# Pooling the keys on VectorE by a strided sum, and splitting and transposing x two blocks ahead in the expert loop

## The chip, the cores and the metric

The kernel runs on one core of one Trainium2 chip. Its engines have their own instruction streams: TensorE (PE, its weight loads are listed as PEld), VectorE (DVE), ScalarE (ACT), GpSimd (POOL) and SyncE (SP), which here only issues transfers. The metric is the device time of one execution in microseconds (us), the median of several runs. Lower is better.

## The reference

Four batches of 12288 queries of 128 channels attend to keys that are pooled from an image of 384 x 32 pixels: each key is the mean of a window of 4 x 4 pixels, so there are 768 keys a batch. The result passes through a mixture of experts: a token whose skip score is positive goes through the expert with the largest gate logit, and the others stay as they are.

```python
kv_pool = kv.reshape(B, H // r, r, W // r, r, C).mean(axis=(2, 4))     # r = 4
kv_flat = kv_pool.reshape(B, -1, C) @ w_sr                             # keys and values
a = softmax(q @ kv_flat.T / sqrt(C));   x = a @ kv_flat                # 49152 rows in all
out = x.copy();   xc = x[x @ w_skip > 0];   e_idx = argmax(xc @ w_gate, axis=1)
for e in range(E):                                                     # 8 experts, F = 1024
    y[e_idx == e] = gate_w * (relu(xc @ w1[e]) @ w2[e])
out[x @ w_skip > 0] = xc + y
```

## The kernel before, in words

**Attention.** 384 tiles of 128 queries, 96 a batch, in an order written out by hand. In each pass of the tile loop the kernel emits, for tile t: the scores of t (`scores`, six matmuls, L580 to L582, into `s_ps`, of which there are two buffers), the product with the values for tile t - 6 (`attend`, L643), the TensorE transposes for t - 1 (L618), the row maximum of t on VectorE (`row_max`, L588), then on ScalarE the high half of the probabilities of t - 1 (`p_hi`, L597) and exp of t (`row_exp`, L593), and on VectorE the low half (`p_lo`, L601), after which SP issues a transfer that transposes both halves. Each product is kept exact by splitting an operand in a high and a low part. After every 12 tiles a job `route` is queued: it works out gate, expert and destination row of 12 x 128 tokens on VectorE and GpSimd (L690 to L774), with two small TensorE matmuls for ranks (L750, L751), and then issues 12 scatters (`scatter_rows`, L184) on GpSimd, two a tile, which write the rows to expert-sorted lists in DRAM (`scr`). GpSimd also makes the low half of the queries once in four tiles (L569).

**Keys of the next batch.** During tiles 0 to about 78 of a batch, SP loads the next batch's image in six blocks of 128 keys (`load_kv`): a block is a tile `kvt` of 128 partitions (one for each key) by 2048 elements, 4 image rows of 4 pixels of 128 channels. Four tiles after a block's last load its pooling (`pool_kv`) joins a queue, `pools`. Blocks join at tiles 13, 26, 39, 52, 65 and 78 of the batch, and each pass of the tile loop takes one step from the queue (two from tile 74 on). A step of `pool_kv` is one GpSimd addition of 128x256, in place, the last one of 128x128: eight additions to a block (L439, L441). At tile 84 `prep_kv` turns the pooled keys into the operands of the next batch. The last batch has no pooling. Writes of padding rows lie in the tiles from 84 on of each batch and throughout the last batch. For the first batch the six blocks are pooled in the prologue: five on VectorE by `pool_kv_first` (a reduce over a strided view in which the 16 pixels of a window are the innermost axis, L426), and block 3 on GpSimd by `pool_kv`.

**The experts.** The first group of 2048 tokens is worked off by `peel`, code without a loop, of which a piece is emitted in each pass after the last attention tile. Then comes a hardware loop (L990) over the other groups. A group is one expert's weights and four blocks (stages) s = 0..3 of 512 tokens. Each block: `up` in eight chunks c (three matmuls each, L266 to L268, then relu in two halves, L269 on ScalarE and L270 on VectorE), `down` (L282), and, in the next block, `finish` (transposes back, L290, addition on VectorE, L293, and four scatters to the output). `x_transpose(s)` splits the rows `xin[s]` into `x16` (one buffer: L253 to L256 of ScalarE and VectorE) and has SP issue a transfer that transposes it into `xT[s]` (L259), from which `up(s)` reads. The loop is staggered: the engines pass from stage to stage at their own pace, and `previous_stage_wait(engine)` marks the place where an engine waits until the previous stage is done on all engines. `load_w` (weights, block 0), `w_scale` (blocks 1 and 2: the weights' scale, 2 reduces of L194 in front), `split_w1` and `split_w2` prepare the next group's weights.

Inside a block the order is: `up` chunk 0; GpSimd and SP wait for the previous stage; chunks 1 to 3; `split_w2` (block 0); `finish` of the previous block; `x_transpose` of the next block; `load_w` (block 0); `load_x` for the previous block's buffer; chunks 4 to 7; the weights' scale and `split_w1`; VectorE and ScalarE wait for the previous stage; `down`.

Of the kernel before, what the change touches and what calls it, by code (L numbers as in the profile page):

```python
# [15 lines left out]
ALU = mybir.AluOpType  # L16
AX = mybir.AxisListType
# [7 lines left out]
def kernel(  # L25
# [11 lines left out]
    nc = tc.nc  # L37
    NR, C, RT, P = q.shape
# [3 lines left out]
    R = 4  # L42
# [4 lines left out]
    FC = FF // P  # L47
# [2 lines left out]
    WEXP = 1  # L50
    W2EXP = 13
    XEXP = 2
    XC = 4
    DL = 1
    K1, K2 = 3, 2
    XP = 3
    XP2 = 4
# [19 lines left out]
    NST = G // ST  # L77
# [89 lines left out]
    op = ctx.enter_context(tc.tile_pool(name="op", bufs=2))  # L167
# [4 lines left out]
    writes, first_writes, finished, ready, loaded, moved = [], [], [], [], [], []  # L172
# [38 lines left out]
    def split_w1(pool=False):  # L211
        nc.scalar.activation(out=w1_hi, in_=w1_raw, func=AF.Copy, scale=w_sc[:, 0:1])
        if pool:
            nc.gpsimd.tensor_scalar(out=w1_raw, in0=w1_raw, scalar1=w_sc[:, 0:1], scalar2=None, op0=ALU.mult)
            nc.gpsimd.tensor_tensor(out=w1_lo, in0=w1_raw, in1=w1_hi, op=ALU.subtract)
            return
        nc.vector.scalar_tensor_tensor(out=w1_lo, in0=w1_raw, scalar=w_sc[:, 0:1], in1=w1_hi, op0=ALU.mult,
                                       op1=ALU.subtract)
# [21 lines left out]
    def split_w2():  # L240
        nc.scalar.activation(out=w2_hi, in_=w2_raw, func=AF.Copy, scale=w_sc[:, 1:2])
        nc.vector.scalar_tensor_tensor(out=w2_lo, in0=w2_raw, scalar=w_sc[:, 1:2], in1=w2_hi,
                                       op0=ALU.mult, op1=ALU.subtract)
        nc.vector.tensor_copy(y_sc[:, 0:1], y_sc[:, 1:2])

    def x_transpose(s, pool=False):
        for t in range(TT):
            nc.scalar.activation(out=x16[:, 0, t, :], in_=xin[s][:, t, 0:C], func=AF.Copy,
                                 scale=xin[s][:, t, C + 2:C + 3])
        if pool:  # L250
            x = op.tile([P, TT, C], F32, name="o")
            nc.gpsimd.tensor_tensor(out=x, in0=xin[s][:, :, 0:C], in1=xin[s][:, :, C + 2:C + 3].broadcast_to([P, TT, C]),
                                    op=ALU.mult)  # L253
            nc.gpsimd.tensor_tensor(out=x16[:, 1, :, :], in0=x, in1=x16[:, 0, :, :], op=ALU.subtract)
        for t in () if pool else range(TT):
            nc.vector.scalar_tensor_tensor(out=x16[:, 1, t, :], in0=xin[s][:, t, 0:C],  # L256
                                           scalar=xin[s][:, t, C + 2:C + 3], in1=x16[:, 0, t, :],
                                           op0=ALU.mult, op1=ALU.subtract)
        nc.sync.dma_start_transpose(xT[s], x16.rearrange("p a t c -> p (a t c)"))  # L259

    def up(s, cs):
        hi, lo = (xT[s][:, i * TT:(i + 1) * TT, :].rearrange("p t x -> p (t x)") for i in range(2))
        for c in cs:
            sl = slice(c * P, (c + 1) * P)
            ps = alloc["h"]()
            nc.tensor.matmul(ps, w1_hi[:, sl], hi, start=True, stop=False)  # L266
            nc.tensor.matmul(ps, w1_hi[:, sl], lo, start=False, stop=False)  # L267
            nc.tensor.matmul(ps, w1_lo[:, sl], hi, start=False, stop=True)  # L268
            nc.scalar.activation(out=h["hi"][:, c, :], in_=ps, func=AF.Relu)  # L269
            nc.vector.scalar_tensor_tensor(out=h["lo"][:, c, :], in0=ps, scalar=0.0, in1=h["hi"][:, c, :],  # L270
                                           op0=ALU.max, op1=ALU.subtract)
# [15 lines left out]
    def finish(s):  # L287
        ps = alloc["x"]()
        for t in range(TT):
            nc.tensor.transpose(ps[:, t * P:(t + 1) * P], yTs[s % 2][:, t * P:(t + 1) * P], ident)  # L290
        o = op.tile([P, TT, C], F32, name="o")
        for t in range(TT):
            nc.vector.scalar_tensor_tensor(out=o[:, t, :], in0=ps[:, t * P:(t + 1) * P],  # L293
                                           scalar=xin[s][:, t, C:C + 1], in1=xin[s][:, t, 0:C],
                                           op0=ALU.mult, op1=ALU.add)
        for t in range(TT):
            scatter_rows(out, xin[s].bitcast(I32)[:, t, C + 1:C + 2], o[:, t, :], NT - 1, "out")
# [41 lines left out]
    def peel():  # L339
        for s in range(NST):  # L340
            for c in range(FC):
                up(s, [c])
                if s == 0 and c == 3:
                    split_w2()
                if s > 0 and c == 3:
                    finish(s - 1)
                    finished.append(s - 1)
                if c == (XP if s < NST - 1 else XP2):
                    x_transpose((s + 1) % NST)
                    if s >= NST - 2:  # L350
                        moved.append(True)
                if s == NST - 1 and c in (1, 3):
                    scale = w_scale() if c == 1 else scale
                    next(scale, None)
                yield
            if s == NST - 1:
                split_w1()
            for i, _ in enumerate(down(s)):
                if s == NST - 1 and i + FC == XP2:
                    x_transpose(0)  # L360
                    moved.append(True)
                yield
            yield

# [2 lines left out]
    with ExitStack() as p1:  # L367
# [47 lines left out]
        def pooled_out(b, k):  # L415
            if k == 0:
                pooled[b] = kprep.tile([P, KC, C], F32, name="pooled")
            return KVT.pop((b, k)), pooled[b][:, k, :]
# [11 lines left out]

        def pool_kv(b, k):
            t, o = pooled_out(b, k)
            f = t.rearrange("p r x -> p (r x)")
            n = R * R * C
            m = 2 * C
            while n > 2 * C:
                n //= 2
                for c in range(0, n, m):
                    nc.gpsimd.tensor_tensor(out=f[:, c:c + m], in0=f[:, c:c + m], in1=f[:, n + c:n + c + m], op=ALU.add)  # L439
                    yield  # L440
            nc.gpsimd.tensor_tensor(out=o, in0=f[:, 0:C], in1=f[:, C:2 * C], op=ALU.add)  # L441

        HK = NK // 2
        HC = KC // 2
# [465 lines left out]
        t = -1  # L910
# [68 lines left out]
    with ExitStack() as p2:  # L979
        alloc_h(p2.enter_context(tc.tile_pool(name="hp", bufs=1)))  # L980
        ps_h = p2.enter_context(tc.tile_pool(name="ps_h", bufs=4, space=PSUM))
        ps_y = p2.enter_context(tc.tile_pool(name="ps_y", bufs=1, space=PSUM))
        ps_x = p2.enter_context(tc.tile_pool(name="ps_x", bufs=2, space=PSUM))

        alloc.update(h=lambda: ps_h.tile([P, ST], F32, name="h_ps"), x=lambda: ps_x.tile([P, ST], F32, name="x_ps"),
                     y=lambda: ps_y.tile([P, ST], F32, name="y_ps"))
        alloc["w"] = alloc["x"]
        tc.prologue_barrier()
        order.__exit__(None, None, None)
        with tc.For_i(0, n_it, 1, hint_engines=(mybir.EngineType.PE,), iteration_sync="staggered") as i:  # L990
            for s in range(NST):
                prv = (s - 1) % NST
                with tc.manual_schedule():
                    up(s, range(0, 1))
                    for eng in (nc.gpsimd, nc.sync):
                        tc.previous_stage_wait(eng.engine)
                    up(s, range(1, 4))
                    if s == 0:
                        split_w2()
                    finish(prv)  # L1000
                    up(s, range(4, XC))
                    x_transpose((s + 1) % NST)
                    if s == 0:
                        load_w(i + 1)
                    load_x(load_start(i if s == 0 else i + 1), prv)
                    up(s, range(XC, FC))
                    if s == 1:
                        scale = w_scale()
                    if s in (1, 2):
                        next(scale, None)  # L1010
                    if s == NST - 1:
                        split_w1()
                    for eng in (nc.vector, nc.scalar):
                        tc.previous_stage_wait(eng.engine)
                    for _ in down(s):
                        pass
                if s < NST - 1:
                    tc.stage_boundary()
        finish(NST - 1)
# [28 lines left out]
```

## Time and profile before

| | |
|---|---|
| median of 3 runs | 1989.95 us (1984.5 to 1991.75) |
| profiled execution | 1995.29 us, span 1992.7 us |
| mean granted TensorE clock | 0.965 |
| PE / DVE / ACT / POOL busy | 90% / 78% / 65% / 55% of the span |
| attention with its prologue, then the first expert group | 0 to about 1116 us, then to about 1209 us |
| expert loop | 1209.6 to about 1985 us |

The span runs from the first to the last instruction. The busy share is that of an engine over the whole span, and the stages differ: attention keeps four engines busy, the expert loop TensorE above all. In a row of a group of instructions stand line, engine, operation, tiles, the count, then the busy time and the mean of one in ns, and then the engine's idle time just before them with what ended most of it; "issue" means that the engine waited for nothing that the profile shows. A row of a table by stage has start and end, length, each engine's busy time with its count of instructions, the granted clock (1.00 is full speed), the share of DMA time and the GB/s moved.

### The profile page before, as it was taken

The numbers are of one execution on the slowest core, as the hardware profiler recorded it, in microseconds if no ns is written. First come the engines' busy times: TensorE is split into PE (matmuls) and PEld (weight loads), VectorE is DVE, ScalarE is ACT, GpSimd is POOL, SyncE is SP. The second block draws the span as 40 slices with busy tenths as digits, with TensorE's granted clock in tenths as the row PEclk, the third lists the DMA queues.
The fourth block names the chain that finished last, engine by engine and source line by source line (L and its number), as shares of the span: only waits on it lengthen the run. The fifth ranks groups of instructions, "written<-read, shape, count | busy, mean of one in ns | idle before, by whom it ended". The sixth has DMA issues, their size and how long they took to land. (4 is left out here: it accounts for less than half of the span.)

```text
span 1992.7 us, 42614 instructions
## 1 busy us (share of the span) xinstructions
PE 1802.1 (90%) x13955; PEld 1284.9 (64%) x13955; DVE 1560.5 (78%) x3222; ACT 1300.6 (65%) x2480; POOL 1095.2 (55%) x1372
## 2 busy tenths in 40 slices
PE   4999989999889998898988768999999999999997
PEld 3988878888878888787877523444444444444443
DVE  7889967999879888776778647777777777777776
ACT  3877867878768877676767534665656556565564
POOL 2378865888757878456556453333343333333334
PEclk9999989999999999888999879999999999999999
DMA  7999978999879999688988523333333333333333
GB/s 178 202 196 211 210 161 178 200 179 191 155 145 188 214 186 210 140 184 176 190 181 174 113 79 86 92 91 90 90 94 107 95 94 88 95 90 93 89 89 90
DMA packets 620915, 284.60 MB, mean 143 GB/s; under 512 B 502113, under 2 KB 570849, under 8 KB 620769
## 3 DMA queue, kind: packets, MB, share of 16 engines
q1 hardware_dynamic: 599264, 244.30, 59.6%
q0 software_dynamic: 21504, 38.43, 6.8%
q8 instruction: 82, 1.34, 0.3%
q14 instruction: 65, 0.52, 0.1%
HBM read 90.60 MB, written 78.64 MB: 85 GB/s over the span
## 5 line engine op out<-in xcount | busy, mean ns | idle before, releaser
L184 POOL DMA_INDIRECT out_dram<-o,xin x288 | 300.3, 1043 | 512.4 <-DVE o L293 435.5
L270 DVE SCALAR_TENSOR_TENSOR h_lo<-h_ps,h_hi 128x512 f16<-128x512 f32 x544 | 343.4, 685 | 174.9 <-ACT h_hi L269 174.9
L588 DVE TENSOR_REDUCE nm<-s_ps 128x1 f32<-128x768 f32 x384 | 363.7, 947 | 138.5 <-PE s_ps L582 73.9
L593 ACT ACTIVATE p_sb<-s_ps,nm 128x768 f32<-128x768 f32 x384 | 347.0, 904 | 187.1 <-DVE nm L588 152.3
L184 POOL DMA_INDIRECT scr<-rows,di x384 | 393.3, 1024 | 137.5 <-issue 108.1
L643 PE MATMUL acc_ps<-v_hi,pt 128*128 128x138 f16 x3072 | 331.5, 228 | 48.9 <-DVE rs L651 23.1
L643 PEld LDWEIGHTS <-pt 128*128 128x128 f16 x4608 | 286.3, 100 | 121.6 <-issue 120.3
L269 ACT ACTIVATE h_hi<-h_ps 128x512 f16<-128x512 f32 x544 | 299.3, 595 | 44.6 <-PE h_ps L268 21.1
L601 DVE SCALAR_TENSOR_TENSOR p<-p_sb,p 128x512 f16<-128x512 f32 x384 | 315.9, 823 | 1.8 <-ACT p L597 0.6
L643 PE MATMUL acc_ps<-v_lo,pt 128*128 128x138 f16 x1536 | 302.6, 227 | 1.0 <-issue 1.0
L580 PE MATMUL s_ps<-k_hi,q_hi 128*128 128x384 f32 x768 | 300.3, 391 | 2.3 <-issue 2.3
L581 PE MATMUL s_ps<-k_lo,q_hi 128*128 128x384 f32 x768 | 266.1, 347 | 4.3 <-issue 4.1
L582 PE MATMUL s_ps<-k_hi,q_lo 128*128 128x384 f32 x768 | 265.6, 346 | 2.6 <-issue 2.6
L597 ACT ACTIVATE p<-p_sb 128x512 f16<-128x512 f32 x384 | 242.4, 631 | 6.0 <-DMA pt<-p 3.0
L266 PE MATMUL h_ps<-xT,w_hi 128*128 128x512 f16 x544 | 206.6, 380 | 26.1 <-issue 26.1
L285 ACT ACTIVATE yT<-y_ps,y_sc 128x512 f32<-128x512 f32 x68 | 46.7, 687 | 276.6 <-PE y_ps L282 212.3
L268 PE MATMUL h_ps<-xT,w_lo 128*128 128x512 f16 x544 | 206.9, 380 | 0.0
L267 PE MATMUL h_ps<-xT,w_hi 128*128 128x512 f16 x544 | 206.8, 380 | 0.0
L282 PE MATMUL y_ps<-h_hi,w_hi 128*128 128x512 f16 x544 | 206.2, 379 | 0.0
L282 PE MATMUL y_ps<-h_hi,w_lo 128*128 128x512 f16 x544 | 206.2, 379 | 0.0
L282 PEld LDWEIGHTS <-w_hi 128*128 128x128 f16 x1152 | 113.3, 98 | 134.3 <-issue 3.7
L282 PE MATMUL y_ps<-h_lo,w_hi 128*128 128x512 f16 x544 | 195.1, 379 | 0.0
(215 smaller groups left out, 3215.0 us busy)
## 6 DMA issues: line engine op xcount, KB each, us to landing
kvt<-in_kv_dram SPq DMA_DIRECT2D x96, 256.0 KB
q_sb<-in_q_dram SPq DMA_DIRECT2D x96, 256.0 KB
out_dram<-rows SPq DMA_DIRECT2D x96, 256.0 KB
xin<-scr SPq DMA_DIRECT2D x75, 264.0 KB, 2.7
w_raw<-in_moe_w_dram SPq DMA_DIRECT2D x38, 512.0 KB, 3.8
scr<-pad SPq DMA_DIRECT2D x32, 264.0 KB
pt<-p SPq DMA_TRANSPOSE x384
scr<-rows,di POOLq DMA_INDIRECT x384
```

Of the source, the lines that this page charges most:

```text
L184: ins = nc.gpsimd.indirect_dma_start(out=dst, out_offset=bass.IndirectOffsetOnAxis(ap=ids, axis=0), in_=src, in_offset=None, bounds_check= ...
L269: nc.scalar.activation(out=h["hi"][:, c, :], in_=ps, func=AF.Relu)
L270: nc.vector.scalar_tensor_tensor(out=h["lo"][:, c, :], in0=ps, scalar=0.0, in1=h["hi"][:, c, :], op0=ALU.max, op1=ALU.subtract)
L282: nc.tensor.matmul(ps, w[:, c, :], h[x][:, c, :], start=(i == 0), stop=(i == len(terms) - 1))
L580: nc.tensor.matmul(s[:, h, :HK], q_hi, k_hi[:, sl], start=True, stop=False)
L581: nc.tensor.matmul(s[:, h, :HK], q_hi, k_lo[:, sl], start=False, stop=False)
L582: nc.tensor.matmul(s[:, h, :HK], q_lo, k_hi[:, sl], start=False, stop=True)
L588: nc.vector.tensor_reduce(out=NM[t], in_=S_PS[t][:, :, :HK], axis=AX.XY, op=ALU.max, negate=True)
L593: nc.scalar.activation(out=P_SB[t], in_=S_PS.pop(t)[:, :, :HK], func=AF.Exp, bias=NM.pop(t))
L597: nc.scalar.activation(out=P16[t][:, 0, :], in_=p_flat(t)[:, 0:KD * P], func=AF.Copy, scale=2.0 ** PEXP)
L601: nc.vector.scalar_tensor_tensor(out=p16[:, 1, :], in0=p_flat(t)[:, 0:KD * P], scalar=2.0 ** PEXP, in1=p16[:, 0, :], op0=ALU.mult, op1=ALU ...
L643: nc.tensor.matmul(ps[:, j % 2, :], w, v[a][:, k, :], start=(i == 0), stop=(i == len(AVL) - 1))
```

## The change

There are three parts. `pool_kv` becomes two VectorE reduces over the strided view, one for each half of the channels, in place of eight GpSimd additions; a block now takes two steps of the queue. In the loop, `x_transpose` is for the block after the next, and is emitted behind chunk 7, after the loads; VectorE's and ScalarE's wait for the previous stage moves up to before chunk 3, and TensorE gets the same wait there. In the peeled group, the x of the loop's second block is split and transposed too, inside the last block's `down`; the test that stood in that place was never true (i + 8 is never 4), and the transpose of the loop's first block stays at chunk 4.

```diff
-    XC = 4
...
             for i, _ in enumerate(down(s)):
-                if s == NST - 1 and i + FC == XP2:
-                    x_transpose(0)
-                    moved.append(True)
+                if s == NST - 1 and i == 1:
+                    x_transpose(1)
                 yield
...
         def pool_kv(b, k):
             t, o = pooled_out(b, k)
-            f = t.rearrange("p r x -> p (r x)")
-            n = R * R * C
-            m = 2 * C
-            while n > 2 * C:
-                n //= 2
-                for c in range(0, n, m):
-                    nc.gpsimd.tensor_tensor(out=f[:, c:c + m], in0=f[:, c:c + m], in1=f[:, n + c:n + c + m], op=ALU.add)
-                    yield
-            nc.gpsimd.tensor_tensor(out=o, in0=f[:, 0:C], in1=f[:, C:2 * C], op=ALU.add)
+            v = t.rearrange("p r (w c) -> p c (r w)", c=C)
+            m = C // 2
+            for c in range(0, C, m):
+                nc.vector.tensor_reduce(out=o[:, c:c + m], in_=v[:, c:c + m, :], axis=AX.X, op=ALU.add)
+                yield
...
                     up(s, range(0, 1))
                     for eng in (nc.gpsimd, nc.sync):
                         tc.previous_stage_wait(eng.engine)
-                    up(s, range(1, 4))
+                    up(s, range(1, 3))
+                    for eng in (nc.vector, nc.scalar, nc.tensor):
+                        tc.previous_stage_wait(eng.engine)
+                    up(s, range(3, 4))
                     if s == 0:
                         split_w2()
                     finish(prv)
-                    up(s, range(4, XC))
-                    x_transpose((s + 1) % NST)
                     if s == 0:
                         load_w(i + 1)
                     load_x(load_start(i if s == 0 else i + 1), prv)
-                    up(s, range(XC, FC))
+                    up(s, range(4, FC))
+                    x_transpose((s + 2) % NST)
                     if s == 1:
                         scale = w_scale()
                     if s in (1, 2):
                         next(scale, None)
                     if s == NST - 1:
                         split_w1()
-                    for eng in (nc.vector, nc.scalar):
-                        tc.previous_stage_wait(eng.engine)
                     for _ in down(s):
                         pass
```

## The prediction

> **What bounds the kernel now.** I read the page's busy times first, then tables of busy time by stage (start and end in us, length, then busy time of PE, PEld, DVE, ACT, POOL, the granted clock, DMA share and GB/s), then groups of instructions, waits and timelines inside the stages that the change touches.
>
> ```profile
> PE 1802.1 (90%) x13955; PEld 1284.9 (64%) x13955; DVE 1560.5 (78%) x3222; ACT 1300.6 (65%) x2480; POOL 1095.2 (55%) x1372
> ```
> ```profile
> 63.30:91.70 28.40, 28.40 (x316) 26.48 (x313) 25.78 (x47) 25.00 (x47) 12.28 (x17) 1.00 0.99 214
> 361.90:514.60 152.70, 143.96 (x1553) 131.91 (x1553) 144.31 (x260) 124.70 (x228) 130.83 (x174) 1.00 0.99 186
> 595.50:783.10 187.60, 175.75 (x1875) 160.72 (x1875) 170.25 (x312) 149.99 (x274) 151.10 (x204) 0.99 1.01 198
> 869.50:1009.50 140.00, 123.55 (x1241) 112.52 (x1240) 104.89 (x208) 100.20 (x182) 79.54 (x109) 0.93 0.91 187
> 291.50:331.40 39.90, 35.05 (x331) 32.19 (x332) 28.82 (x61) 26.37 (x48) 21.18 (x29) 0.88 0.86 168
> 557.00:595.50 38.50, 33.15 (x329) 29.85 (x330) 28.22 (x63) 26.21 (x48) 21.51 (x30) 0.96 0.82 159
> 253.40:265.60 12.20, 8.16 (x61) 7.19 (x59) 4.91 (x11) 4.75 (x10) 9.32 (x15) 0.72 0.84 162
> 521.40:533.30 11.90, 7.28 (x61) 6.42 (x61) 5.17 (x10) 4.78 (x10) 9.42 (x15) 0.86 0.63 122
> ```
>
> PE is the first limit: 90% busy, and the first row is twelve attention tiles at 28.40 us with PE busy all the time, 2.37 us a tile. I call twelve tiles (one routing job, twelve scatters) a row. The second and third lines are five and six rows in which GpSimd also pools the next batch's keys: 340.30/11 = 30.94 us a row, POOL and DVE nearly full. The fourth is four rows of the last batch, with no pooling: 35.00 us a row although POOL is busy only 57%, and the clock falls to 0.93. The next two are the first rows of batches 1 and 2, before pooling starts: 39.2 us on average. So in this kernel the rows *without* pooling are the slow ones, and the first question is why.
>
> Two stretches of GpSimd's timeline (start, us, then the instruction), and the waits of TensorE that fall behind the first:
>
> ```profile
> 891.69 1.08 POOL L184 DMA_INDIRECT scr<-rows,di  x1 [0.52 <-issue]
> 893.07 0.97 POOL L184 DMA_INDIRECT scr<-rows,di  x1 [0.30 <-issue]
> 894.35 0.97 POOL L184 DMA_INDIRECT scr<-rows,di  x1 [0.31 <-issue]
> 895.62 0.97 POOL L184 DMA_INDIRECT scr<-rows,di  x1 [0.30 <-issue]
> 896.89 0.98 POOL L184 DMA_INDIRECT scr<-rows,di  x1 [0.30 <-issue]
> 898.18 0.97 POOL L184 DMA_INDIRECT scr<-rows,di  x1 [0.30 <-issue]
> ```
> ```profile
> 386.82 0.97 POOL L184 DMA_INDIRECT scr<-rows,di  x1 [0.30 <-issue]
> 387.80 0.76 POOL L439 TENSOR_TENSOR kvt<-kvt 128x256 f32<-128x256 f32 x1
> 388.72 0.99 POOL L184 DMA_INDIRECT scr<-rows,di  x1 [0.17 <-issue]
> 390.02 0.97 POOL L184 DMA_INDIRECT scr<-rows,di  x1 [0.30 <-issue]
> 391.01 1.22 POOL L439 TENSOR_TENSOR kvt<-kvt 128x256 f32<-128x256 f32 x1
> ```
> ```profile
> 897.55 0.33 PE L580 MATMUL s_ps<-k_hi,q_hi 128*128 128x384 f32 x1 [1.03 <-issue]
> 899.25 0.67 PE L581 MATMUL s_ps<-k_lo,q_hi 128*128 128x384 f32 x1 [0.84 <-issue]
> ```
>
> Without pooling, six scatters follow one another every 1.28 us, and some 5 us after the run began TensorE stands still by pieces, put down to nothing that the profile shows. With pooling, each pair of scatters has an addition (L439) behind it, and no such stop follows. The profile does not say what the scatters hold up; that runs of six and stops go together is what I build on.
>
> The expert loop, from its first matmul to the end of its last block (17 groups of four blocks):
>
> ```profile
> 1209.61:1978.80 769.19, 746.62 (x3561) 354.80 (x3562) 589.46 (x1326) 452.96 (x917) 282.74 (x271) 1.00 0.36 93
> ```
> ```profile
> PE h_ps L266 <- issue: 26.1, 35, 3.5
> ```
> ```profile
> 1490.87 1.25 SPq L259 DMA_TRANSPOSE xT<-x  x1
> 1505.80 0.29 DVE L195 TENSOR_SCALAR w_dg<-ident,w_max 128x128 f32<-128x128 f32 x1
> ```
> ```profile
> 1494.45 0.38 PE L266 MATMUL h_ps<-xT,w_hi 128*128 128x512 f16 x1 [0.58 <-issue]
> 1506.13 0.38 PE L266 MATMUL h_ps<-xT,w_hi 128*128 128x512 f16 x1 [0.72 <-issue]
> ```
>
> TensorE is the bound here: 22.6 us idle of 769. The idle time sits at the first up matmul of a block (35 waits, 26.1 us, the 3.5 us of loop entry included): twice a group, once because the transpose of the next block's x was issued only 3.58 us before the block starts (1490.87 to 1494.45), once right after DVE's weight-scale work (1505.80), behind which stands DVE's wait for the previous stage.
>
> **The change, part by part.** My sum is made against the profiled run, 1995.29 us for a span of 1992.7; the median of the runs is 1989.95, so I subtract 5.3 at the end.
>
> *The additions that GpSimd loses.* The groups of the pooling stage 361.9 to 514.6, GpSimd first, then VectorE's there and (last) in the stage without pooling:
>
> ```profile
> L184 POOL DMA_INDIRECT scr<-rows,di x58 | 60.7, 1047 | 16.8 <-issue 12.1 <-POOL rows L774 4.4 <-PE acc_ps L643 0.2
> L439 POOL TENSOR_TENSOR kvt<-kvt 128x256 f32<-128x256 f32 x32 | 27.3, 860 | 0.2
> ```
> ```profile
> L601 DVE SCALAR_TENSOR_TENSOR p<-p_sb,p 128x512 f16<-128x512 f32 x60 | 54.8, 914 | 0.0
> ```
> ```profile
> L601 DVE SCALAR_TENSOR_TENSOR p<-p_sb,p 128x512 f16<-128x512 f32 x48 | 35.5, 740 | 0.0
> ```
>
> Each of the 18 blocks pooled inside the tile loop gives up seven additions of 0.86 us and one smaller, some 6.5 us of GpSimd. They all leave the path if GpSimd is not the bound, and they take two things with them. First, the gaps between the pairs of scatters. Pooling stood in 18 rows; the first (63.30 to 91.70, 17 POOL instructions) has hardly a scatter yet, so 17 rows lose their gaps. If these become like the rows without pooling, each costs 35.00 - 30.94 = 4.06 us more by the last batch's rows, or 39.2 - 30.94 = 8.3 by the first rows of batches 1 and 2. The latter carry the same key loads as the rows in question, but also the start of a batch; I take 4.06, since I can't take the start out of the others, and keep 8.3 for the range: 17 x 4.06 = **+69** (0 if GpSimd's run does no harm there; to +140). Second, VectorE's p_lo is 914 ns beside the additions and 740 without: 12 x 0.174 = 2.1 us of VectorE a row. That gain is already inside the 35.00.
>
> The Trainium skill ("SBUF — State Buffer", section "Who interferes with whom") says that a VectorE instruction with two SBUF inputs contends with a GpSimd instruction that reads SBUF, while a reduce never does. The 914 against 740 ns agree; taken alone, the rule would make the change a gain, which is rival B.
>
> *The reductions that VectorE gains.* The nearest rows are the reduces over the same strided view in the prologue:
>
> ```profile
> L426 DVE TENSOR_REDUCE pooled<-kvt 128x128 f32<-128x2048 f32 x3 | 10.8, 3596 | 8.3 <-DMA kvt<-in_kv_dram 8.3
> L426 DVE TENSOR_REDUCE part<-kvt 128x128 f32<-128x1024 f32 x2 | 3.8, 1898 | 0.4 <-DMA kvt<-in_kv_dram 0.4
> ```
>
> The new ones read 1024 elements a partition each, so 1.90 us, two to a block, in consecutive tiles. VectorE has 104.89/48 = 2.19 us of work per tile without pooling, TensorE needs 2.37: 0.18 to spare. Two reduces put VectorE 3.80 - 0.36 = 3.4 us behind. Behind them wait the row maximum (L588), then ScalarE's exp, then the free score buffer that TensorE needs. There are two such buffers, so TensorE can run about one tile's work ahead; with 2.1 us of lead, 1.3 us of the 3.4 shows: 17 x 1.3 = **+22** (0 to 3.4 x 17 = 58).
>
> By the Trainium skill ("VectorE: DVE Perf Modes", "The perf-mode tier table") a 1x pass over 2048 fp32 elements takes 2293 ns, so half of it about 1.15 us, an estimate; the row says 1.90 for this strided view, and by the page this term would be near nothing.
>
> *GpSimd no longer late at the end of a batch.*
>
> ```profile
> PE misc L750 <- POOL oh_all L723: 4.0, 1, 4.0
> ```
>
> In 253.40 to 265.60, two tiles took 12.20 us instead of 4.74 (11.90 in 521.40 to 533.30): TensorE's rank matmul waits 4.0 us for GpSimd, which is late from pooling, and the pipeline behind it empties. The same stop stands once in each of three batches. With pooling gone GpSimd is in time: 3 x 7 = **-21** (-22 to 0, if the routing is late for another reason).
>
> *The prologue's block.*
>
> ```profile
> 18.02 4.95 POOL L439 TENSOR_TENSOR kvt<-kvt 128x256 f32<-128x256 f32 x7 [13.14 <-DMA kvt<-in_kv_dram]
> ```
>
> This work ran beside VectorE's own reduces, which follow each other there with waits of 0.4 us; on VectorE it is two reduces of 1.90 in the chain to the first scores: **+3.5** (0 to 3.8).
>
> *The loop.* Issued a block earlier, the transposes are off the path, and the previous-stage wait no longer stands behind the weight scale. At stake is all idle time at L266 but the entry: 26.1 - 3.5 = 22.6, with a little at the weight loads, so **-22** (0 to -28). Against it: SP now issues the transpose behind the x load, and the single x16 buffer is held by the transpose of the block before, so ScalarE and VectorE can wait for it; SP's queue also carries the weight loads. *The entry:* a second transpose in the last peeled block needs rows that are loaded late:
>
> ```profile
> 1205.09 1.65 SPq L190 DMA_DIRECT2D xin<-scr  x2
> 1209.61 0.38 PE L266 MATMUL h_ps<-xT,w_hi 128*128 128x512 f16 x1 [3.49 <-issue]
> ```
>
> ```profile
> xin<-scr SPq DMA_DIRECT2D x75, 264.0 KB, 2.7
> ```
>
> The load (2.7 us from issue to landing, after 1205.09), the split and the transpose (3.58) end near 1212, so +3 once (0 to 5).
>
> Sum: 69 + 22 - 21 + 3.5 - 22 + 3 = +54.5; 1995.3 + 54.5 - 5.3 = **2044**.
>
> **The rivals.** **B, relief wins** (the other side): the scatters' run does no harm in these rows, because it hurts only where something else of the slow rows is there too (padding writes or a batch start). Then 69 is 0, and half of the 2.1 us of VectorE a row reaches TensorE: 22 - 17 x 1.05 = +4, with -21, -22 and +6.5: -32.5, **1957**. Its floor is VectorE full: 12 x 2.19 + 3.8 = 30.1 a row against 30.94, so -14 in place of +4: 1939. For it: POOL is 86% busy and p_lo slow in pooling rows. Against: of the two kinds of row without pooling one has key loads and the other has padding, and both stop. It decides from a run price under 1.9 us a row (32.5/17). **C, VectorE becomes the bound:** no harm from the runs, but the two reduces cost their full 3.4: 17 x (3.4 - 1.05) = +40 for +4, so +3.5: **1993**. The Trainium skill ("VectorE: DVE Perf Modes", "Rules for kernel authors") speaks for it: it calls the reduce the slowest VectorE operation on a hot path and advises restructuring. **D, the loop does not do what it says:** the forecast with its 22 us lost to the x16 buffer or SP's order: 2044 + 22 = **2066**.
>
> **Chances.** Forecast 0.49, D 0.10, B 0.28, C 0.13. Within 0.5% (10 us, about what a measurement of this kernel can tell from no change) lie 0.08 of C; the rest of C is split evenly. Faster 0.28 + 0.025 = 0.305, same 0.08, slower 0.49 + 0.10 + 0.025 = 0.615. The forecast's own range is 2008 (half the run's price) to 2085 (40 more, a run price of 6.4); B must be held down to 1950, and I leave out its lower third (0.09) and the dearest end of the run's price with D (0.1): 1950 to 2085.
>
> **What would show it.** Right: GpSimd's timeline shows runs of six scatters in 361 to 515, the same five rows take 175 or more instead of 152.7 with POOL less busy, and the granted clock dips there. B: those rows at 30 to 31 us each, no stop behind six scatters. C: ScalarE's exp waiting long for L588 beside the new reduces with no run near. The new reduces should read about 1.9 us; PE's wait for L723 should be gone; idle time at L266 should drop to the entry's. Wrong at the root I would be if the pieces of idle TensorE time in the last batch stem from something that the scatters only accompany.

## The result

The changed kernel takes 2064.15 us (median of 4 runs, 2063.22 to 2078.57), the kernel before 1990.85 (1984.5 to 1998.91): 3.85% slower, a ratio of 1.0385 with a 95% interval of [1.0335, 1.0436]. The forecast was 2044, between 1950 and 2085, slower. The profiled execution took 2078.57 us for a span of 2076.7, against 1995.29 and 1992.7.

One thing is needed to read the numbers behind this. The four later comparisons each set their kernels against the kernel before on one chip, and each met another chip. On two of these the kernel before took 1893 to 1895 us, on the other two 1992 and 2002, as in the first pair. What differs between them is the main finding of the experiments: in the second kind TensorE stops behind runs of scatters. I call them chips without and chips with stops. The names are for the condition alone: chip and time changed together from one comparison to the next, so the runs do not tell whether the condition belongs to the chip.

The busy times of the page after, and the table by stage of the changed kernel (columns as in the prediction: start and end, length, then PE, PEld, DVE, ACT, POOL, clock, DMA share, GB/s):

```profile
PE 1836.3 (88%) x13955; PEld 1315.3 (63%) x13955; DVE 1597.7 (77%) x3264; ACT 1328.5 (64%) x2484; POOL 966.0 (47%) x1220
```
```profile
365.30:595.40 230.10, 193.51 (x1903) 176.11 (x1901) 181.76 (x324) 151.34 (x277) 126.19 (x173) 0.92 0.78 152
670.70:897.90 227.20, 193.27 (x1886) 174.56 (x1885) 179.97 (x325) 150.69 (x275) 125.76 (x170) 0.92 0.82 166
973.50:1116.50 143.00, 127.79 (x1273) 116.74 (x1271) 105.14 (x210) 101.82 (x187) 83.62 (x116) 0.92 0.90 185
```

The first two rows are six rows of twelve tiles each with pooling, in batches 1 and 2: 38.35 and 37.87 us a row, where before it was 30.54 and 31.27. They now look like the third, the four rows of the last batch without pooling (35.75, before 35.00). The granted clock is 0.92 in all three. Every engine has a smaller share of the span than before. GpSimd's timeline in one run of scatters, then TensorE's instructions behind it that had to wait:

```profile
1033.53 1.07 POOL L183 DMA_INDIRECT scr<-rows,di  x1 [0.52 <-issue]
1034.91 0.97 POOL L183 DMA_INDIRECT scr<-rows,di  x1 [0.31 <-issue]
1036.18 0.97 POOL L183 DMA_INDIRECT scr<-rows,di  x1 [0.30 <-issue]
1037.45 0.97 POOL L183 DMA_INDIRECT scr<-rows,di  x1 [0.30 <-issue]
1038.73 0.97 POOL L183 DMA_INDIRECT scr<-rows,di  x1 [0.30 <-issue]
1040.00 0.97 POOL L183 DMA_INDIRECT scr<-rows,di  x1 [0.30 <-issue]
```
```profile
1039.31 0.27 PE L612 MATMUL acc_ps<-ident,p_sb 128*128 128x128 f32 x1 [1.02 <-issue]
1040.74 0.43 PE L576 MATMUL s_ps<-k_hi,q_lo 128*128 128x384 f32 x1 [0.80 <-issue]
1043.94 0.39 PE L637 MATMUL acc_ps<-v_hi,pt 128*128 128x138 f16 x2 [2.25 <-DVE rs L645]
```

These are the stops of the forecast. From the fourth scatter of the run on, TensorE halts twice between two matmuls of the same tile, for no reason that the profile shows; its third wait, of 2.25 us, is put down to VectorE's `rs`. TensorE is not the only engine that stands still:

```profile
1042.24 0.96 DVE L582 TENSOR_REDUCE nm<-s_ps 128x1 f32<-128x768 f32 x1 [5.49 <-PE s_ps L576]
```

By the order of the instructions this row maximum is that of the scores whose last matmul began at 1036.71 and took 0.34 us. VectorE starts it 5.2 us after that, and `rs` stands behind it. ScalarE has waited 3.97 us when it goes on at 1040.78. Behind the stop TensorE is slow as well: the granted clock is 1.00 from 1036.00 to 1038.00 and 0.52 from 1044.00 to 1047.00, and the pairs of L637 take 0.44 us there in place of 0.28.

The rest of the change as it came out is in the following lines. VectorE's pooling group and its low halves of the probabilities in 365 to 595; then the first scores' row maximum, before and after; then the loop's first and last block (the last of the kernel before, then both of the changed one, and its entry wait):

```profile
L434 DVE TENSOR_REDUCE pooled<-kvt 128x64 f32<-128x1024 f32 x12 | 23.4, 1953 | 0.0
...
L595 DVE SCALAR_TENSOR_TENSOR p<-p_sb,p 128x512 f16<-128x512 f32 x72 | 55.5, 771 | 0.0
```
```profile
34.28 0.96 DVE L588 TENSOR_REDUCE nm<-s_ps 128x1 f32<-128x768 f32 x1
```
```profile
37.80 0.96 DVE L582 TENSOR_REDUCE nm<-s_ps 128x1 f32<-128x768 f32 x1
```
```profile
1970.02 0.38 PE L266 MATMUL h_ps<-xT,w_hi 128*128 128x512 f16 x1
```
```profile
1319.64 0.58 PE L265 MATMUL h_ps<-xT,w_hi 128*128 128x512 f16 x1 [7.42 <-issue]
...
2052.18 0.38 PE L265 MATMUL h_ps<-xT,w_hi 128*128 128x512 f16 x1
```
```profile
PE h_ps L265 <- issue: 7.4, 1, 7.4
```

The reduce reads 1.95 us, p_lo 771 ns in place of 914, the prologue is 3.52 us longer, and the loop from its first to its last block takes 2052.18 - 1319.64 = 732.54 us instead of 1970.02 - 1209.61 = 760.41: 27.87 less. The only wait left at the first up matmul in the loop is its entry's. The loop starts 1319.64 - 1209.61 = 110.03 us later than before: 3.52 of it from the prologue and 7.42 - 3.49 = 3.93 from the entry, so 102.6 from the attention's tiles and the first expert group. That is where the time went. The profiled execution is the longest of the changed kernel's, 14 us above the median, so its stages are somewhat dearer than those of a usual one.

### The profile page after: what moved, and what is told of

It reads as the page before. It is cut to its first block, busy times and chain, and to the rows that moved or that the text cites. A ratio compares the mean times of both kernels' runs of the same rounds, so it can differ in the third digit from the quotient of the medians.

```text
span 2076.7 us, 42615 instructions
## 1 busy us (share of the span) xinstructions
PE 1836.3 (88%) x13955; PEld 1315.3 (63%) x13955; DVE 1597.7 (77%) x3264; ACT 1328.5 (64%) x2484; POOL 966.0 (47%) x1220
## 5 line engine op out<-in xcount | busy, mean ns | idle before, releaser
L183 POOL DMA_INDIRECT out_dram<-o,xin x288 | 295.7, 1027 | 494.6 <-DVE o L292 428.4
L637 PE MATMUL acc_ps<-v_hi,pt 128*128 128x138 f16 x3072 | 343.0, 233 | 108.9 <-DVE rs L645 67.0
L637 PEld LDWEIGHTS <-pt 128*128 128x128 f16 x4608 | 297.2, 102 | 189.9 <-issue 189.1
L268 ACT ACTIVATE h_hi<-h_ps 128x512 f16<-128x512 f32 x544 | 318.3, 597 | 51.1 <-PE h_ps L267 31.9
L637 PE MATMUL acc_ps<-v_lo,pt 128*128 128x138 f16 x1536 | 311.7, 232 | 4.7 <-issue 4.6
L574 PE MATMUL s_ps<-k_hi,q_hi 128*128 128x384 f32 x768 | 306.2, 399 | 4.5 <-issue 4.3
L595 DVE SCALAR_TENSOR_TENSOR p<-p_sb,p 128x512 f16<-128x512 f32 x384 | 289.9, 755 | 1.6 <-ACT p L591 1.0
L576 PE MATMUL s_ps<-k_hi,q_lo 128*128 128x384 f32 x768 | 270.0, 352 | 6.2 <-issue 6.2
L563 POOL TENSOR_TENSOR q_lo<-q_sb,q_hi 128x512 fp32r<-128x512 f32 x96 | 123.8, 1290 | 236.5 <-ACT q_hi L562 236.2
L637 PE MATMUL acc_ps<-v_hi,ptq 128*128 128x138 f16 x1536 | 189.6, 230 | 7.8 <-issue 7.5
```

What stands on the lines that cost most here:

```text
L183: ins = nc.gpsimd.indirect_dma_start(out=dst, out_offset=bass.IndirectOffsetOnAxis(ap=ids, axis=0), in_=src, in_offset=None, bounds_check= ...
L574: nc.tensor.matmul(s[:, h, :HK], q_hi, k_hi[:, sl], start=True, stop=False)
L576: nc.tensor.matmul(s[:, h, :HK], q_lo, k_hi[:, sl], start=False, stop=True)
L595: nc.vector.scalar_tensor_tensor(out=p16[:, 1, :], in0=p_flat(t)[:, 0:KD * P], scalar=2.0 ** PEXP, in1=p16[:, 0, :], op0=ALU.mult, op1=ALU ...
L637: nc.tensor.matmul(ps[:, j % 2, :], w, v[a][:, k, :], start=(i == 0), stop=(i == len(AVL) - 1))
```

## The experiments

My theory, R, was that runs of scatters stop TensorE and that GpSimd's additions had kept them apart. Its rival, V, was that the two reduces on VectorE cost the time and the scatters only accompany the stops.

**The parts alone.** The first kernel is the one before with the loop's part of the change, the second with the pooling's part.

```diff
 e1: before + x_transpose((s + 2) % NST) behind chunk 7, the moved waits, x_transpose(1) in the peeled group
 e2: before + pool_kv as two nc.vector.tensor_reduce a block
```

> The kernel before with the loop's part of the change alone (x two blocks ahead, the waits moved, the second transpose in the peeled group); keys still pooled on GpSimd. In the trace of the changed kernel the 67 block starts of the loop span 732.5 us instead of 760.4, and the loop's entry waits 7.4 us instead of 3.5. If the two parts add, this kernel is 28 - 4 = 24 us faster than before: about 1967. If the loop only runs faster because VectorE or the queues are left in another state by the attention, it is within 10 us of 1991.

> The kernel before with the pooling's part alone, prologue included. If the two parts add, 2064 + 24 = 2088. Below 2075 the parts would not be independent.

This was a chip without stops: the kernel before took 1893.54. The loop's part took 1869.31, ratio 0.9871 [0.9854, 0.9887], 24.2 us faster; the pooling's part 1922.52, ratio 1.015 [1.0133, 1.0167], 29.0 us slower. The loop's part is worth the 24 that were expected. The pooling's part costs 29 us instead of the nearly 100 expected from the first pair, and its rows without pooling, like those of the first kernel, don't stop. The two kernels by stage, six rows with pooling (the first kernel's second row: four rows without):

```profile
313.60:498.10 184.50, 174.80 (x1895) 160.79 (x1893) 176.48 (x313) 149.36 (x277) 160.24 (x211) 1.00 1.00 194
822.90:940.90 118.00, 115.93 (x1262) 107.06 (x1260) 108.43 (x210) 100.07 (x186) 84.36 (x113) 1.00 1.09 222
```
```profile
326.90:526.50 199.60, 179.50 (x1899) 165.28 (x1897) 185.18 (x325) 150.67 (x278) 132.09 (x174) 0.97 0.91 181
```

Here a row costs 30.75 us with GpSimd's pooling, 33.27 with VectorE's and 29.50 with none. The exchange of poolings costs 33.27 - 30.75 = 2.5 us a row, by the same rows of two kernels. Against the rows without pooling VectorE's two reduces cost 33.27 - 29.50 = 3.8 us a row, nearly all of their 3.9 us, so no sign is left that the two score buffers hide any of it; GpSimd's additions cost 1.25. These two figures are less sure, since the rows without pooling also lack the key loads and have writes of padding rows.

**One scatter a tile, and filler additions.** Both change the spacing of the scatters in the changed kernel and leave its reduces as they are.

```diff
 e3: after, with 4 buffers for rowp in place of 3 (SNAPR is 27)
-                if j % 2 == 0 and j > 0 and r < LASTR - 1:
+                if (j > 0 if r < SNAPR else j % 2 == 0 and j > 0) and r < LASTR - 1:
                     yield
 e4: after, with two scratch tiles junk
...
                 if j % 2 == 0 and j > 0 and r < LASTR - 1:
+                    nc.gpsimd.tensor_tensor(out=junk[0], in0=junk[0], in1=junk[1], op=ALU.add)   # 128x256
                     yield
```

> The changed kernel with one scatter a tile in place of two (a step of the routing job behind each scatter, in the first 27 rows; one more buffer for rows, since a row is held longer). Theory R (runs of scatters stop TensorE): the runs of six are gone, and with them a stop of about 5.7 us in each of 27 rows (tile of 7.5 us and a slow one of about 3 behind it, against 2 x 2.37): 2064 - 27 x 5.7 = 1910, between 1890 and 1960. Theory V (the two reduces delay TensorE, the scatters only accompany): the reduces are as before, so 2064, 2050 to 2075.

> The changed kernel with one GpSimd addition of 128x256 on a scratch tile behind each pair of scatters (some 0.75 us, as the pooling had there), nothing else. It adds work. Theory R: the gaps are back, the stops go: at most 1980, by 27 rows x 4 us or more below 2064, less 10 to 20 for the contention with VectorE that the additions bring back. Theory V: GpSimd's additions only cost, 2064 to 2090.

On the same chip as the parts, one scatter a tile took 1891.57, ratio 0.9987 [0.9978, 0.9997], and the filler 1967.06, ratio 1.0377 [1.0357, 1.0397]. The expectations were made against 2064, and on this chip there was nothing of the stops to remove. That both times lie where theory R put them is an accident, and neither decides between the theories. What the second shows is the price of the additions themselves, some 69 us above the 1893.5 - 24.2 + 29.0 = 1898 that the parts add up to. Its waits in four rows of the last batch,

```profile
PE misc L747 <- POOL oh_all L720: 13.3, 4, 3.5
```

say that TensorE now waits 3.3 us in each row for a GpSimd that is late with the routing. Whether such additions would remove more than that on a chip with stops was not run.

**The changed kernel again.** It is run unaltered, to see whether the slowdown itself comes back.

> The changed kernel itself, unaltered. In the trace of the pooling's part alone, twelve tiles of the last batch took 29.5 us behind the same runs of six scatters, not 35.0, and the kernel before took 1893.5 us instead of 1991 in that comparison. Theory R1 (the stops behind runs belong to the condition in which the first pair was measured): where the kernel before takes about 1893, this one is the sum of the parts, 1893.5 + 29.0 - 24.2 = 1898, ratio 1.003; where it takes about 1990, ratio 1.038 again. Theory R2 (the stops come only with both parts together): about 2064 or a ratio of 1.038 in either condition.

Another chip without stops: before 1894.52, the changed kernel 1897.82, ratio 1.0015 [1.0005, 1.0025]. That is the sum of the parts (1898) to within a microsecond, and theory R2 falls. Its table (six rows with pooling, four without) and one run of scatters:

```profile
325.60:525.10 199.50, 179.74 (x1898) 165.59 (x1896) 185.22 (x325) 150.45 (x278) 132.86 (x174) 0.97 0.93 180
851.30:969.20 117.90, 115.84 (x1260) 106.96 (x1258) 108.47 (x209) 99.87 (x185) 84.30 (x113) 1.00 1.09 221
```
```profile
907.13 0.97 POOL L183 DMA_INDIRECT scr<-rows,di  x1 [0.31 <-issue]
908.40 0.97 POOL L183 DMA_INDIRECT scr<-rows,di  x1 [0.30 <-issue]
909.67 0.97 POOL L183 DMA_INDIRECT scr<-rows,di  x1 [0.30 <-issue]
```

The run of scatters is the same, 1.27 us apart, and TensorE is busy 115.84 of the 117.90 us around it. The same program and the same run of scatters stop TensorE on one chip and not on another. The first line gives the price of the stops in one and the same program: 199.50 us here against 230.10 in the first pair, 5.1 us a row. TensorE's busy time differs by 193.51 - 179.74 = 13.8 us, so 2.3 of the 5.1 us a row are slower work and 2.8 are standing still.

**Sizes without the stops.** Three more kernels were compared on that chip.

```diff
 e6: e1 (keys pooled on GpSimd) + one scatter a tile, as in e3
 e7: after
-            m = C // 2
+            m = C // 4                                      # four reduces of 512 elements in four tiles
 e8: e1, with the last block of each batch (k == KC - 1) pooled by VectorE's two reduces
```

> Keys pooled on GpSimd, the loop's part of the change, and one scatter a tile in the first 27 rows. Where the kernel before takes about 1893 there are no stops to remove: as the loop's part alone, 1869, 1860 to 1875. Where it takes about 1990, theory R says that the stops of the 8 rows of batches 1 to 4 that have no pooling and are spread go: 8 x 5.7 = 46 less than the loop's part alone, 1920; if runs don't matter, 1967.

> The changed kernel with four reduces a block over a quarter of the channels (512 elements a partition, 1.02 us by the prologue's row) in four tiles, in place of two of 1.9 us in two tiles. If bursts cost (a reduce too long for the slack of its tile), each tile now falls behind by about 0.8 us in place of 1.7, and the two score buffers take up part of it: 10 to 30 us less than the changed kernel. If the sum of VectorE's work sets the pace (4 x 1.02 is 0.3 us more a block), the same within 6 us.

> The loop's part of the change, keys pooled on GpSimd but for the last block of each batch, which goes to VectorE by two reduces. If GpSimd is late at the batch's end because of that last block, the stop of TensorE at the ranks goes (about 5 to 7 us in each of three batches) for a cost of 3.8 us each: 1869 - 3 x 1.5 to 3 x 3 = 1860 to 1865 where the loop's part alone takes 1869. If the lateness has built up over the earlier blocks, the stop stays and the cost remains: 1875 to 1880.

Quarters took 1878.25, ratio 0.9919 [0.9902, 0.9936], 19.6 us less than halves. So the length of one reduce matters and not only the sum of them, which rose from 2 x 1.95 to 4 x 1.05 us a block. Six rows with pooling, and the group of reduces in 330 to 480:

```profile
317.00:510.00 193.00, 176.67 (x1905) 161.84 (x1903) 184.24 (x338) 150.35 (x279) 130.76 (x172) 1.00 0.96 186
```
```profile
L434 DVE TENSOR_REDUCE pooled<-kvt 128x32 f32<-128x512 f32 x17 | 17.9, 1053 | 0.0
```

193.00/6 = 32.17 us a row against 33.25; 18 rows make the 19.6. But 32.17 - 29.50 = 2.7 of the 3.8 us a row stay. One scatter a tile with GpSimd's pooling took 1864.06, ratio 0.9842 [0.9825, 0.9858], within its expectation and the fastest kernel measured on a chip without stops. The last block on VectorE took 1873.47, ratio 0.9887 [0.9864, 0.9911], 4 us more than the loop's part alone, which ran on the other chip without stops, and between the two expectations. Tiles 72 to 83 and 84 to 95, first of this kernel, then of the loop's part alone:

```profile
214.40:251.40 37.00, 31.29 (x314) 28.72 (x312) 32.91 (x55) 24.65 (x45) 31.05 (x39) 0.91 0.94 180
251.40:285.00 33.60, 31.53 (x336) 28.62 (x332) 29.31 (x58) 27.18 (x53) 19.16 (x28) 1.00 1.00 200
```
```profile
214.10:244.90 30.80, 28.95 (x315) 26.52 (x313) 29.27 (x54) 24.44 (x45) 26.72 (x36) 1.00 1.05 193
244.90:283.70 38.80, 33.18 (x335) 29.82 (x332) 30.46 (x58) 27.12 (x53) 29.30 (x39) 0.96 0.87 188
```

The stop at the end of the batch is gone (33.60 against 38.80), and the row of the reduces pays it back (37.00 against 30.80), with a new wait of TensorE of 4.9 us for VectorE's `rs`. So GpSimd was late there because of the last block.

**Longer and shorter runs where there are stops.** The next comparison met a chip with stops (before 1992.13), so that theory R could be put to the test.

```diff
 e9: after
-                if j % 2 == 0 and j > 0 and r < LASTR - 1:
+                if j % 4 == 0 and j > 0 and r < LASTR - 1:   # four scatters a tile
 e10: e6, a block pooled by 4 GpSimd additions (half on half) and then 4 reduces of 256 elements on VectorE
 e11: e3 with
-            m = C // 2
+            m = C // 8                                      # eight reduces of 256 elements in eight tiles
```

> The changed kernel with four scatters a tile in place of two, so that up to twelve follow one another. In the second comparison (kernel before 1894.5) the changed kernel's runs of six did not stop TensorE. Theory L (a stop comes once a run is long enough, and the first pair's condition only lowered that length): runs of twelve bring stops of 5 us or more in about 27 rows, 1898 + 135 = 2030 or more; half of the rows, 1965. Theory N (in this condition runs of scatters don't stop TensorE, however long): 1898, 1885 to 1910.

> The loop's part of the change and one scatter a tile, with the pooling shared: GpSimd adds the halves of a block (four additions of 128x256), VectorE then sums the remaining 8 pixels in four reduces over a quarter of the channels (256 elements a partition, half of the 1.02 us of 512, an estimate), eight steps to a block as before. If rows with pooling are paced by GpSimd's lateness in one kernel and by VectorE's bursts in the other, halving both gives about 30 us a row: 1864 (loop's part and one scatter a tile) - 18 x 0.8 = 1850. If what costs is VectorE's total, 2.0 us more a block than with GpSimd alone: 1864 + 20 to 36 = 1884 to 1900.

> The changed kernel with one scatter a tile and eight reduces a block over an eighth of the channels (256 elements). Quarters took 19.6 us less than halves, one scatter a tile 6 less. If the burst's length is what costs, eighths fall short of a tile's slack by only 0.3 us each: 1878 - 6 - 5 to 10 = 1862 to 1867. If VectorE's sum of 4.2 us a block or more sets the pace: 1872 to 1878.

The expected times were for a chip without stops, so none of them can be held against these runs, and the rows decide. Whether runs of twelve would stop TensorE on a chip without stops, which theories L and N were about, stays open. Longer runs took 2132.39, ratio 1.0681 [1.0634, 1.0728], where the changed kernel has 1.0385. Four rows without pooling, and one run of scatters with TensorE's restarts behind it:

```profile
1017.30:1167.10 149.80, 131.16 (x1258) 115.88 (x1257) 104.44 (x209) 101.04 (x184) 81.26 (x113) 0.91 0.84 176
```
```profile
1047.19 0.97 POOL L183 DMA_INDIRECT scr<-rows,di  x1 [0.30 <-issue]
1048.47 0.97 POOL L183 DMA_INDIRECT scr<-rows,di  x1 [0.30 <-issue]
1049.75 0.97 POOL L183 DMA_INDIRECT scr<-rows,di  x1 [0.30 <-issue]
1051.03 0.97 POOL L183 DMA_INDIRECT scr<-rows,di  x1 [0.30 <-issue]
```
```profile
1048.00 0.28 PE L637 MATMUL acc_ps<-v_hi,pt 128*128 128x138 f16 x2 [0.96 <-issue]
...
1049.36 0.28 PE L637 MATMUL acc_ps<-v_hi,pt 128*128 128x138 f16 x2 [0.50 <-issue]
...
1050.77 0.28 PE L637 MATMUL acc_ps<-v_hi,ptq 128*128 128x138 f16 x2 [1.07 <-issue]
...
1052.20 0.28 PE L637 MATMUL acc_ps<-v_hi,ptq 128*128 128x138 f16 x1 [1.03 <-issue]
```

A row without pooling takes 37.45 us here, 1.7 more than in the first pair with runs of six. TensorE restarts every 1.4 us, once behind the start of each of the four scatters, 0.8 to 1.2 us later: between two of them it does a few matmuls of one tile and stops again.

One scatter a tile with eighths took 1929.23, ratio 0.968 [0.9639, 0.9722]. Six rows with pooling and four without:

```profile
319.60:513.70 194.10, 176.78 (x1887) 160.63 (x1884) 182.37 (x361) 150.73 (x277) 131.20 (x170) 1.00 0.98 183
840.40:960.80 120.40, 115.78 (x1260) 106.92 (x1258) 111.48 (x209) 101.11 (x185) 87.57 (x113) 1.00 1.10 218
```

The last row is the cleanest test of the cause. In these four rows of the last batch no keys are pooled, so the reduces play no part; the only edits that act there are the scatters' spacing and the fourth buffer for rows. A row takes 30.10 us with the clock back at 1.00, where it took 35.75 in the first pair and 37.45 with the longer runs on this same chip, and TensorE has no wait there that is put down to nothing. The same trace holds the counter-test: from row 27 on the kernel still issues two scatters a tile, the fourth buffer is there too, and six scatters 1.27 us apart follow one another from 1022.22. TensorE stops again:

```profile
1025.16 0.28 PE L637 MATMUL acc_ps<-v_hi,pt 128*128 128x138 f16 x2 [1.79 <-issue]
1030.02 0.22 PE L637 MATMUL acc_ps<-v_lo,ptq 128*128 128x138 f16 x1 [1.30 <-issue]
1031.42 0.58 PE L612 MATMUL acc_ps<-ident,p_sb 128*128 128x128 f32 x2 [1.18 <-issue]
```

So it is not the buffer. On a chip with stops they come with the runs of scatters, and theory V falls there.

The shared pooling took 1967.07, ratio 0.9856 [0.9816, 0.9895]: 1.4% faster than before, but far behind eighths on the same chip. VectorE's reduces now queue behind GpSimd's additions. In 604 to 745:

```profile
DVE pooled L439 <- POOL kvt L434: 6.2, 3, 3.4
```

Three blocks made VectorE wait up to 3.4 us with the row maximum behind it. Whether that is all of the 38 us to the other kernel stays open.

**The best of them again.** The kernel of eighths was repeated unaltered.

> The same kernel as the run of eighths with one scatter a tile, unaltered, for a comparison in which the kernel before may take another time. Where the kernel before takes about 1893 there are no stops to remove, and only the shorter reduces and the small gain of one scatter a tile act: 1898 - 6 - 20 - 5 = 1867, 1858 to 1876, ratio 0.986. Where it takes about 1992: 1929 again, ratio 0.968.

It met another chip with stops, with 2001.99 before: 1935.6, ratio 0.9677 [0.9641, 0.9713], the expected ratio. So this version beats both kernels by over 3% on chips with stops; on one without it was not measured, and there the kernel with GpSimd's pooling and one scatter a tile, at 0.9842, is the best that was.

## Why the prediction was right, and what in it was not

In the profiled executions the change cost 2078.57 - 1995.29 = 83.3 us, and the sum had 54.5. The rows with pooling, below, make 122 where 91 was forecast. With -17 at the ends of the batches, 3.5, -27.9 and 3.9 for the other terms they add up to 85, so no term of this size is missing.

**The runs of scatters: right, and near the right size.** The term was 17 x 4.06 = 69. The rows with pooling grew by 38.35 - 30.54 = 7.8 and 37.87 - 31.27 = 6.6 us, 7.2 on average; 2.5 of it is what the exchange of poolings costs without stops (33.27 - 30.75), which leaves 4.7, or 80 for 17 rows. The same program with and without stops gives 5.1 for the first six rows, so the size does not rest on that difference alone. The step "runs of six and stops go together is what I build on" held where the first pair was measured, and on another chip with stops spacing the scatters removed them in the rows of the last batch. What it lacked: it took the stops for a property of the program. On two chips they are absent, and on the one of these on which the changed kernel ran it is at 1.0015, where the sum of the prediction makes 1.027. The forecast holds for the condition that its trace was taken in.

**The reductions: the mechanism right, the size too small.** The step that failed is "with 2.1 us of lead, 1.3 us of the 3.4 shows". No row stands behind the lead of 2.1 us and no run shows it: without stops a row pays 3.8 us, nearly all of both reduces. In the first pair a row with pooling was 38.1 against 35.75 without: 2.4 where 1.3 was forecast, so 17 x 1.1 = 19 us. With the 11 us by which the runs' term was short, that is the 31 us that the rows cost more than the forecast; the loop's larger gain took 6 of them back. That 2.4 and not 3.8 shows in rows with stops is not explained by any run. Rival C was right where there are no stops: it put the change at 3.5 us, and there it is 1897.82 - 1894.52 = 3.3, because VectorE's reduces take back what the loop gives. The length of one reduce is part of their price: a row pays 3.8 us with halves, 2.7 with quarters and, in the run of eighths, (194.10/6) - (120.40/4) = 2.25 on a chip with stops. More than half stays, while the sum of VectorE's work grows. The Trainium skill ("VectorE: DVE Perf Modes", "Rules for kernel authors") calls the reduce the slowest VectorE operation on a hot path and advises restructuring. The 3.8 us for two reduces of 1.95 us agree; the runs show that shorter pieces answer it in part.

**GpSimd late at the end of a batch: right.** The two tiles that took 12.20 us:

```profile
294.20:300.70 6.50, 5.42 (x60) 4.88 (x59) 4.70 (x11) 5.02 (x11) 1.31 (x4) 1.00 1.18 210
```

They take 6.50, so 5.7 is gained and not the 7 that were reckoned: 17 in place of 21, if the ends of the other two batches gain the same. TensorE's wait for `oh_all`, 21.7 us in 12 waits over the attention before, does not occur in the changed kernel's.

**The prologue: right**, 3.5 forecast and 3.52 measured. **The entry: right**, 3 forecast and 3.93. **The loop: right in its mechanism, at the upper end**: 22 forecast with a bound of 28, 27.9 measured. All of the 22.6 us of idle time went, and TensorE's busy time fell by some 5 us for the same work (737.84 to 732.54 us from the first to the last block). An estimate of why: in a row the matmuls start 0.215 us apart, but the last one in front of a wait is recorded with its full 0.38 us, so each of the 34 waits cost about 0.16 us more than its idle time shows, 5.6 us in all. Rival D fell: neither the x16 buffer nor SP's order took anything back.

**Rival B** fell in the first pair, on the condition I gave: rows at 38 us, not 30 to 31. On the chips without stops its premise was right (the runs do no harm), but the relief did not pay: 33.27 us a row against 30.75. The Trainium skill's rule of two SBUF inputs ("SBUF — State Buffer", "Who interferes with whom") is borne out by p_lo, which fell from 914 to 771 ns in the first pair with the additions gone. On the chip of the parts it fell from 938 to 807, but VectorE gained 12 x 0.131 = 1.6 us a row by it and was given 3.9.

## What to carry to other kernels

Work that is taken off an engine can have been pacing another stream on it: look at what then follows back to back, in the stages of the same profile that already lack that work. An operation on the engine that feeds the critical one is priced by the length of one piece as well as by the total: shorter pieces lowered the price here, from 3.8 to 2.7 us a row, but did not remove it. A slowdown that rests on an unexplained wait should be measured on more than one chip before a design is chosen by it.

## What the runs showed that was not expected

The stops came on some chips alone. With the same program and its scatters 1.27 us apart on both, a row without pooling took 35.75 us in the first pair and 117.90/4 = 29.48 on a chip without stops. Where they come, TensorE halts once behind each scatter late in a run, about 1 us in the lines shown, between matmuls that depend on nothing new, and VectorE and ScalarE stand still in the same stretch; GpSimd's scatters go on. What the scatter holds up was not found: the profile puts most of it down to nothing, and whether it belongs to the chip or to what else ran at that time was not tried. What is shown is that the stops come and go with the runs of scatters on one chip, in one trace.
